# Hash-masked attention and a gated feed-forward layer on one core: value blocks 144 bytes apart, 128-row scores for ten head pairs, a new order of a few steps, and one more unit turned by DMA

## The chip, the core and the metric

The kernel runs on one NeuronCore of a Trainium2 chip. Five engines work side by side, each on its own in-order list of instructions: TensorE (PE in the profile, with its weight loads shown apart as PEld), VectorE (DVE), ScalarE (ACT), GpSimd (POOL) and SyncE (SP), which here only issues DMAs. They meet through semaphores. SBUF is the on-chip memory of 128 partitions, PSUM holds the matmul results, and DMAs move data between the external memory and SBUF or within SBUF. The metric is the device time of one execution in microseconds; of several executions the median counts.

## The reference

The input is q, k and v of shape 4 x 8 x 768 x 64 (batch, heads, tokens, head size), a projection of 64 x 6, and the weights of a feed-forward layer. All are float32, and the output is float32 of shape 3072 x 512. Cut to what matters:

```
q_bits = (q @ proj) > 0;  k_bits = (k @ proj) > 0            # six bits each
mask   = bucket(q_bits)[:, None] == bucket(k_bits)[None, :]   # same bucket only
scores = where(mask, q @ k.T / sqrt(64), -1e9)
attn   = exp(scores - max);  attn = attn / (sum(attn) + 1e-9)
x      = heads of (attn @ v) side by side                     # 3072 x 512
xn     = x / sqrt(mean(x * x) + 1e-6) * rms_g
out    = (silu(xn @ w_gate) * (xn @ w_val)) @ w_out           # 512 -> 1536 -> 512
```

## The kernel before, in words

**Units and slots.** The work is cut into eight units `w`: half of the tokens (384) of one batch `b = w // 2`. A unit's attention goes over 8 heads `h`, two heads forming a pair `hp`; its feed-forward part goes over 12 blocks `ft` of 128 of the 1536 hidden features. A list SLOTS (lines 33 to 36) holds 192 slots; a slot is one third of a head's scores, two blocks of 128 keys against 384 queries. Units 0 and 1 take turns by pairs, then units 2 and 3; units 4 to 7 follow one by one. A plan written out by hand (`at(slot, function, ..., rank=...)`, from line 595) puts every other step into a slot, and the loop from line 731 emits slot after slot: the next slot's scores, the steps with a rank below 3, the exponentials, then the other steps by rank. Each engine executes its own part in the order of this emission, so a step that waits holds up everything behind it on its engine.

**Scores.** For each pair a tile QK of 128 partitions holds, per head, the keys and the queries with the 64 head dimensions on partitions 0 to 63. Partitions 64 to 75 hold 12 rows of scaled hash bits, which make the matmul itself subtract a large number where the buckets differ, so KROWS = 76 rows are contracted (`k_cols`, `q_cols`, lines 146 to 157). The QK tiles come from a pool of six buffers (line 67). Rows 0 to 63 are written by casts (mostly on POOL, `cast_pool` and `cast_half`); the bit rows come by small DMAs on the SP queue or by copies on DVE. `scores` (line 343) issues two matmuls of 384 columns per slot, `probs` the exponential on ACT.

**Values.** `v_prep` (line 312) casts the values on POOL into the tile `vl` of shape 128 x 8 heads x 6 blocks x 66 in 16 bits, so one block starts 132 bytes after the one before; column 64 of each is one, which yields the sum of the exponentials. `av` (line 362) issues 18 matmuls per head, each with 65 columns of one such block moving, in two halves of nine. `v_sum` and `v_mean` form the mean of the values, from which `attn_out` takes the 1e-9 term.

**Output and norm.** `attn_out` (line 378; called through `o_step`) adds that term and divides on DVE, multiplies into x and squares, both on POOL; only for unit 0's last pair (`urgent`, line 392) do both run on DVE. `sumsq` (through `s_step`) sums the squares on DVE; `norm` (line 415) goes DVE, POOL, POOL. `scale_x` (DVE) and `turn_x` bring x into the layout for the next matmuls: for units in BY_DMA, here 3, 4 and 5, the first two of three chunks are turned by eight DMA transposes on the SP queue (line 441), otherwise by four TensorE transposes per chunk and a DVE multiplication (lines 448 and 449).

**Feed-forward.** Unit `w` starts its gate and value matmuls (lines 463 and 473) at slot 24w + 42 and its output matmuls (`project`, line 486) 16 slots later. `bank` hands out three PSUM banks for everything but scores and attention outputs: gates, values, output rows, transposes, hash products and value means all take their turn in them. A matmul into a bank waits until the engine that reads its former content has done so.

**Queue of SP.** All loads of q, k and v, the bit rows, the DMA transposes and the output rows are issued on the SP queue in the order of the plan. The weights are loaded from the POOL queue.

**The end.** The last 128 output rows are computed in two halves of 256 columns (lines 743 to 759): the first is copied by ACT and stored from SP; of the second ACT copies 128 columns and DVE the other 128 of the same bank, and ACT and SP store them.

## Time and profile before

| what | value |
| --- | --- |
| time, median of 3 runs | 334.26 us (334.0, 334.26, 335.18) |
| span of the profiled execution, first to last instruction | 332.5 us |
| time of the profiled execution itself | not listed apart from the three; the span is 1.8 us below their median |
| TensorE busy | 323.3 us, 97% of the span |
| VectorE, ScalarE, GpSimd busy | 234.2, 208.0 and 157.1 us (70%, 63%, 47%) |
| mean granted TensorE clock | 0.998 |
| DMA | 32.41 MB in 89956 packets |

How to read it: "busy" is the time in which at least one instruction of an engine was running. Matmuls overlap, so the duration of one (325 ns with 384 columns) is longer than the distance from its start to the start of the next. A group row of the profile gives line, engine, operation, tiles and shapes, count, then busy time in us and the mean of one in ns, then the idle time of the engine before these instructions and what ended it. A row of a timeline gives start and length in us; several like instructions in a row are merged, with their count. A row of a view by stretches gives the limits, the length, the busy time and count of each engine, the granted clock, the share of DMA time and GB/s. SPq rows are the issue of DMAs by SP, not their transfer.

### The profile page before, as it was taken

The page shows a single profiled execution, that of the slowest core. Times are in us where ns is not written, and L with a number is a line of the kernel's source. Part 1 is how long each engine was busy: PE and PEld are TensorE (multiplying, and loading weights), DVE is VectorE, ACT ScalarE, POOL GpSimd, SP SyncE. Part 2 cuts the span into 40 slices and gives each one's busy share as a digit, 9 for nine tenths or more (in the row PEclk, how much of TensorE's full clock was granted, in tenths as well). Part 3 has the DMA queues.
Part 4 walks back from the last instruction along what each step waited for, and adds up shares of the span by engine and source line. Part 5 has one row for each costly group of instructions (what it writes and reads, how often), then busy time and mean ns, then how long its engine had stood idle before and what let it go on. Part 6 is the DMA issues. An engine that isn't in the chain of part 4 may idle for free.

```text
span 332.5 us, 7788 instructions
## 1 busy us (share of the span) xinstructions
PE 323.3 (97%) x2959; PEld 198.5 (60%) x2959; DVE 234.2 (70%) x526; ACT 208.0 (63%) x324; POOL 157.1 (47%) x230
## 2 busy tenths in 40 slices
PE   8999989998999999999999999999999999999995
PEld 7576656555566556656565656566566656655653
DVE  3799579997598956989476874977257753793860
ACT  3788977674576665667675766757666766422421
POOL 4887956487747476376744365643110311130000
PEclk9999999999999999999999999999999999999999
DMA  6995997898348927841361714000200001002002
GB/s 221 349 201 151 147 173 140 158 172 134 117 86 156 168 40 174 156 90 24 91 146 34 141 34 150 3 17 18 80 32 2 3 32 65 0 3 82 13 2 95
DMA packets 89956, 32.41 MB, mean 97 GB/s; under 512 B 75336, under 2 KB 86848, under 8 KB 89920
## 3 DMA queue, kind: packets, MB, share of 16 engines
q1 hardware_dynamic: 85984, 27.14, 35.0%
q0 software_dynamic: 3712, 4.72, 9.2%
q8 instruction: 23, 0.38, 0.5%
q14 instruction: 13, 0.11, 0.1%
q10 hardware_dynamic: 224, 0.07, 0.1%
HBM read 28.58 MB, written 6.29 MB: 105 GB/s over the span
## 4 chain that ended last, share of the span: by engine, by line
PE 82%; DVE 5%; DMA 5%; POOL 4%; ACT 1%; issue 1%; SPq 1%; POOLq 0%; DVEq 0%; ACTq 0%
PE v_ps L473 17%; PE y_ps L486 16%; PE s_ps L348 15%; PE g_ps L463 14%; PE o_ps L370 9%; PE s_ps L463 4%; PE d_ps L214 3%; DMA QK<-bits 3%; PE t_ps L174 2%; DMA kL<-in_k_dram 1%; PE z_ps L341 1%; PE x_ps L448 1%; DVE t L474 1%; PE y_ps L747 1%; POOL sq L406 1%
## 5 line engine op out<-in xcount | busy, mean ns | idle before, releaser
L358 ACT ACTIVATE psb<-s_ps 128x768 f16<-128x768 f32 x192 | 150.6, 809 | 31.9 <-PE s_ps L348 29.9
L348 PE MATMUL s_ps<-QK 76*128 76x384 f16 x384 | 93.7, 325 | 2.5 <-DMA QK<-bits 1.3
L473 PE MATMUL v_ps<-xnT,wv 128*128 128x384 f16 x384 | 78.1, 325 | 0.0
L486 PE MATMUL y_ps<-wo,ht 128*128 128x512 f16 x276 | 69.2, 378 | 0.0
L394 POOL TENSOR_TENSOR x<-otmp,rcp 128x384 f32<-128x384 f32 x31 | 26.1, 843 | 84.8 <-DVE rcp L390 84.6
L370 PEld LDWEIGHTS <-psb 128*128 128x128 f16 x1152 | 52.2, 97 | 22.0 <-issue 3.6
L465 ACT ACTIVATE t<-g_ps 128x384 f32<-128x384 f32 x78 | 38.3, 491 | 43.2 <-PE g_ps L463 42.7
L463 PE MATMUL g_ps<-xnT,wg 128*128 128x384 f16 x312 | 63.4, 325 | 0.3
L474 DVE SCALAR_TENSOR_TENSOR t<-t,g_ps 128x384 f32<-128x384 f32 x78 | 42.7, 547 | 28.8 <-ACT t L465 28.4
L475 DVE SCALAR_TENSOR_TENSOR ht<-t,v_ps 128x384 f16<-128x384 f32 x96 | 53.2, 554 | 10.4 <-PE v_ps L473 0.9
L370 PE MATMUL o_ps<-vl,psb 128*128 128x65 f16 x1152 | 56.7, 193 | 0.3 <-DVE otmp L385 0.3
L463 PEld LDWEIGHTS <-wg 128*128 128x128 f16 x384 | 36.0, 97 | 24.1 <-issue 0.7
L473 PEld LDWEIGHTS <-wv 128*128 128x128 f16 x384 | 36.2, 97 | 23.2
L348 PEld LDWEIGHTS <-QK 76*128 76x128 f16 x384 | 31.3, 98 | 19.3 <-issue 4.7
L486 PEld LDWEIGHTS <-ht 128*128 128x128 f16 x276 | 26.0, 97 | 26.3 <-issue 1.9
L493 ACT COPY ysb<-y_ps 128x512 f32<-128x512 f32 x23 | 13.5, 587 | 24.6 <-PE y_ps L486 24.1
L406 POOL TENSOR_TENSOR sq<-x 128x384 f32<-128x384 f32 x31 | 26.3, 849 | 2.4
L385 DVE TENSOR_TENSOR otmp<-o_ps,cvb 128x390 f32<-128x390 f32 x32 | 17.9, 559 | 12.6 <-PE o_ps L370 12.5
L206 POOL CAST QK<-qT 64x768 f16<-64x768 f32 x22 | 18.1, 823 | 15.8 <-DVE qT L198 15.1
L206 POOL CAST QK<-kT 64x768 f16<-64x768 f32 x22 | 18.5, 841 | 13.6 <-PE m_ps L329 3.8
L449 DVE TENSOR_TENSOR xnT<-x_ps,gcol 128x512 f16<-128x512 f16 x18 | 12.2, 683 | 14.1 <-PE x_ps L448 14.0
L198 DVE STREAM_TRANSPOSE kT<-kL 128x192 f32<-128x192 f32 x44 | 21.7, 515 | 0.0
(81 smaller groups left out, 297.6 us busy)
## 6 DMA issues: line engine op xcount, KB each, us to landing
vL<-in_v_dram SPq DMA_DIRECT2D x16, 384.0 KB
out_dram<-ysb SPq DMA_DIRECT2D x23, 256.0 KB
kL<-in_k_dram SPq DMA_DIRECT2D x44, 96.0 KB
qL<-in_q_dram SPq DMA_DIRECT2D x44, 96.0 KB
kL<-in_k_dram SPq DMA_DIRECT2D x4, 384.0 KB
qL<-in_q_dram SPq DMA_DIRECT2D x4, 384.0 KB
wg<-in_moe_w_gate_dram POOLq DMA_DIRECT2D x2, 768.0 KB, 8.2
wv<-in_moe_w_val_dram POOLq DMA_DIRECT2D x2, 768.0 KB, 9.3
```

The costliest lines, as they stand in the source:

```text
L206: nc.gpsimd.tensor_copy(QK[b, hp][0:64, hh, o : o + S], T0[b, hp, which][64 * hh : 64 * hh + 64, :])
L348: nc.tensor.matmul(ps[:, j, 0:HALF], k_cols(w // 2, h, 2 * p + j), q_cols(w, h), start=True, stop=True,)
L358: nc.scalar.activation(psb[w, h][:, p], sps.pop(g)[:, :, 0:HALF], AF.Exp, scale=ESCALE,)
L370: nc.tensor.matmul(o[:, c, hh, 0:65], psb[w, h][:, jt // 2, jt % 2, 128 * c : 128 * c + 128], vls[b % 2][:, h, v_chunk(b, h, jt), 0:65], s ...
L394: eng.tensor_mul(xd.rearrange("p c (h d) -> p c h d", h=2), tmp[:, :, :, 0:64], r.to_broadcast([128, 3, 2, 64]),)
L406: nc.gpsimd.tensor_mul(sq, xd, xd)
L463: nc.tensor.matmul(g, wg[:, kt, fs], xnT[w][:, kt], start=(kt == 0), stop=(kt == 3))
L465: nc.scalar.activation(t, g, AF.Tanh, scale=0.5)
L473: nc.tensor.matmul(vv, wv[:, kt, fs], xnT[w][:, kt], start=(kt == 0), stop=(kt == 3))
L474: nc.vector.scalar_tensor_tensor(out=t, in0=t, scalar=1.0, in1=g, op0=ALU.add, op1=ALU.mult)
L475: nc.vector.scalar_tensor_tensor(out=ht[w][:, ft], in0=t, scalar=0.5, in1=vv, op0=ALU.mult, op1=ALU.mult)
L486: nc.tensor.matmul(y, ht[w][:, ft, c * 128 : (c + 1) * 128], wo[:, ft, :], start=(ft == 0), stop=(ft == NF - 1),)
```

## The change

- VSTEP = 72: the value blocks in `vl` lie 72 elements, 144 bytes, apart instead of 132. Reads still take 65 of them.
- The QK tiles are six fixed tiles `qkbuf` used in rotation, instead of six buffers of a pool. `clear_rows` sets partitions 64 to 127 of one of them to zero on POOL (a memset of 64 partitions x 1536 words): for buffers 4 and 5 at the start, behind the other memsets, and for buffers 2, 3, 0 and 1 in slots 76, 78, 97 and 98.
- For the ten pairs (1,0), (1,1) and all of batches 2 and 3, scores are contracted over all 128 rows instead of 76. Pairs of batch 0 and (1,2), (1,3) keep 76.
- `urgent` now covers unit 0's pairs 2 and 3: pair 2's multiplication and squares move from POOL to DVE, and its `s_step` goes.
- `s_step` of unit 6's last pair comes one slot earlier, and its `norm` two (slot 173 instead of 175).
- Unit 6 joins BY_DMA: chunks 0 and 1 are scaled in slots 175 and 176 together with the gain row, and are turned by eight DMA transposes on the SP queue in the same slots.
- `v_prep` and `v_sum` of pair (2,1) come two slots later (84 instead of 82), behind the norm of unit 2, which is planned in slot 83.
- `v_mean` of pairs 0 and 1 in batches 2 and 3 comes four slots earlier (88 instead of 92, and 136 instead of 140).
- The last 128 rows are computed in pieces of 256, 128 and 128 columns, each in a bank of its own. ACT copies and stores the first two; DVE copies the third, and SP stores it.

```
+VSTEP = 72
-BY_DMA = (3, 4, 5)
+BY_DMA = (3, 4, 5, 6)
-    qkpool = ctx.enter_context(tc.tile_pool(name="qkpool", bufs=6))
-    vls = [const.tile([128, H, 6, 66], FP16, name=f"vl{i}") for i in range(2)]
+    vls = [const.tile([128, H, 6, VSTEP], FP16, name=f"vl{i}") for i in range(2)]
+    qkbuf = [const.tile([128, 2, 2 * S], FP16, name=f"QK{i}") for i in range(6)]
-            QK[b, hp] = qkpool.tile([128, 2, 2 * S], FP16, name="QK")
+            QK[b, hp] = qkbuf[len(QK) % len(qkbuf)]
+    def clear_rows(i):
+        nc.gpsimd.memset(qkbuf[i][D:128].rearrange("p h n -> p (h n)").bitcast(FP32), 0.0)
+    def score_rows(b, hp):
+        return slice(0, 128 if (b, hp) in ((1, 0), (1, 1)) or b > 1 else KROWS)
-        return QK[b, h // 2][0:KROWS, h % 2, o : o + 128]
+        return QK[b, h // 2][score_rows(b, h // 2), h % 2, o : o + 128]
-        t = QK[b, h // 2][0:KROWS, h % 2]
+        t = QK[b, h // 2][score_rows(b, h // 2), h % 2]
-        urgent = (w, hp) == (0, 3)
+        urgent = (w, hp) in ((0, 2), (0, 3))
...
+    clear_rows(4)
+    clear_rows(5)
...
-        at(cast_slots[2], v_prep, b, hp)
-        at(cast_slots[2], v_sum, b, hp)
+        late = 2 if (b, hp) == (2, 1) else 0
+        at(cast_slots[2] + late, v_prep, b, hp)
+        at(cast_slots[2] + late, v_sum, b, hp)
         if b > 1 and hp % 2:
-            at(48 * b + (17 if hp == 3 else -4), v_mean, b, hp - 1, 4)
+            at(48 * b + (17 if hp == 3 else -8), v_mean, b, hp - 1, 4)
+    for i, s in ((2, 76), (3, 78), (0, 97), (1, 98)):
+        at(s, clear_rows, i, rank=6)
...
-                if (w, h) != (0, 7):
-                    late = 3 if h == 7 and w < 6 else 5 if (w, h) == (0, 5) else 4
-                    at(end + late, s_step, w, h // 2, rank=5 if late != 5 else 4)
+                if (w, h) not in ((0, 5), (0, 7)):
+                    late = 3 if h == 7 and w < 7 else 4
+                    at(end + late, s_step, w, h // 2, rank=5)
-        n0 = {0: 11, 2: 7, 3: 13, 4: 13, 5: 13}.get(w, 11)
+        n0 = {0: 11, 2: 7, 3: 13, 4: 13, 5: 13, 6: 13}.get(w, 11)
...
-    for i in range(2):
-        cs = slice(256 * i, 256 * i + 256)
+    for lo, hi in ((0, 256), (256, 384), (384, 512)):
         y = bank("y_ps")
...
+        copy, queue = (nc.vector.tensor_copy, nc.sync) if hi == 512 else (nc.scalar.copy, nc.scalar)
+        copy(ysb[:, lo:hi], y[:, lo:hi])
+        queue.dma_start(out=rows[:, lo:hi], in_=ysb[:, lo:hi])
```

More of the change, by code (lines that the diff above doesn't have):

```diff
@@ L747 @@
             nc.tensor.matmul(
-                y[:, cs], ht[7][:, ft, 256:384], wo[:, ft, cs],
+                y[:, lo:hi], ht[7][:, ft, 256:384], wo[:, ft, lo:hi],
                 start=(ft == 0), stop=(ft == NF - 1),
@@ L751 @@
         ysb = spool.tile([128, DMODEL], FP32, name="ysb", bufs=3)
-        if i == 0:
-            nc.scalar.copy(ysb[:, 0:256], y[:, cs])
-            nc.sync.dma_start(out=rows[:, cs], in_=ysb[:, 0:256])
-        else:
-            nc.scalar.copy(ysb[:, 0:128], y[:, 256:384])
-            nc.vector.tensor_copy(ysb[:, 128:256], y[:, 384:512])
-            nc.scalar.dma_start(out=rows[:, 256:384], in_=ysb[:, 0:128])
-            nc.sync.dma_start(out=rows[:, 384:512], in_=ysb[:, 128:256])
+        copy, queue = (nc.vector.tensor_copy, nc.sync) if hi == 512 else (nc.scalar.copy, nc.scalar)
+        copy(ysb[:, lo:hi], y[:, lo:hi])
+        queue.dma_start(out=rows[:, lo:hi], in_=ysb[:, lo:hi])
 _INS = ['q', 'k', 'v', 'proj', 'moe_w_gate', 'moe_w_val', 'moe_w_out', 'moe_rms_g']
```

## The prediction

> **What bounds the kernel now.** I read the page's busy times first, then the view by stretches, then what TensorE waits for.

> ```profile
> PE 323.3 (97%) x2959; PEld 198.5 (60%) x2959; DVE 234.2 (70%) x526; ACT 208.0 (63%) x324; POOL 157.1 (47%) x230
> 46.00:76.60 30.60, 29.33 (x283) 17.82 (x280) 27.43 (x64) 20.36 (x32) 20.60 (x29) 1.00 0.87 154
> 76.60:122.00 45.40, 44.76 (x409) 26.45 (x410) 34.31 (x78) 28.91 (x44) 28.67 (x39) 1.00 0.60 117
> 122.00:285.00 163.00, 162.71 (x1493) 98.86 (x1492) 111.50 (x235) 108.70 (x168) 70.73 (x92) 1.00 0.30 67
> ```

> The first numbers behind the length are TensorE's. From 76.6 us to 285 us it stands idle for 0.93 us in all, and no other engine comes near it: work taken off TensorE there shortens the run by its full amount. Before 76.6 us that does not hold:

> ```profile
> 75.27 0.44 PE L370 MATMUL o_ps<-vl,psb 128*128 128x65 f16 x9
> 76.65 0.48 PE L348 MATMUL s_ps<-QK 76*128 76x384 f16 x2 [0.94 <-DMA QK<-bits]
> 64.41 0.68 DVE L221 TENSOR_SCALAR bits<-d_ps,thr,scl 128x384 f16<-128x384 f32 x1
> 68.61 0.58 SPq L116 DMA_DIRECT2D vL<-in_v_dram  x1
> 69.29 6.20 SPq L289 DMA_DIRECT2D QK<-bits  x8
> 70.99 5.53 DMA QK<-bits
> ```

> The nine attention matmuls that start at 75.27 are streamed by 75.55 (31 ns each, below), and the next scores start at 76.65: 1.1 us of waiting for the hash bits of pair (1,1). DVE had these bits at 65.09, but SP is behind with loads and reaches their DMAs only at 69.29; the third, issued at 70.99, lands 5.53 us later. SP and the transfers set this moment, not TensorE. What TensorE gains ahead of it only lengthens the wait, and I count nothing of it.

> **The value blocks.** Mean distance between attention matmuls after 76.6 us (first row: those of line 370 alone):

> ```profile
> 76.60:332.50 255.90, 40.54 (x819) 37.62 (x819) 1.00 0.31 70
> 77.84 0.43 PE L370 MATMUL o_ps<-vl,psb 128*128 128x65 f16 x9
> L370 PE MATMUL o_ps<-vl,psb 128*128 128x65 f16 x1152 | 56.7, 193 | 0.3 <-DVE otmp L385 0.3
> L448 PE MATMUL x_ps<-ident,xn 128*128 128x128 f16 x72 | 7.0, 219 | 1.2 <-DVE xn L434 1.2
> ```

> 819 matmuls are 91 runs of nine like the second row; a run is eight distances and one duration of 193 ns, so a distance is (40.54 - 91 x 0.193) / 728 = 31.6 ns. The transposes, in 18 runs of four, give (7.0 - 18 x 0.219) / 54 = 56.6 ns for 128 columns, 28.7 ns for 65. Sorted by where the block starts, the single start times behind the first row say the same: 29.2 ns from a block whose address is a multiple of 16 bytes (each fourth), mostly 32 to 35 ns from the others. With 144 bytes all are multiples. 819 x (31.6 - 29.2) = 1.9 us, all on TensorE after 76.6; 0 if the address is not the reason, 819 x (31.6 - 28.7) = 2.4 at most. I take 1.9, the value that the aligned blocks show now.

> **128-row scores.** A matmul's length does not depend on the rows:

> ```profile
> L348 PE MATMUL s_ps<-QK 76*128 76x384 f16 x384 | 93.7, 325 | 2.5 <-DMA QK<-bits 1.3 <-ACT psb L358 0.8 <-ACT qT L182 0.2
> L473 PE MATMUL v_ps<-xnT,wv 128*128 128x384 f16 x384 | 78.1, 325 | 0.0
> ```

> Both last 325 ns. But in the start times behind these rows the first matmul of a score pair takes 165 to 167 ns to the next start and the first one after the pair 3 to 4 ns above its usual distance, where steps between other 128-row groups cost nothing. Per pair that is 7.6 ns; 108 of the 132 pairs after 76.6 us change to 128 rows: 0.8 us. I take it; the other end is 0, if the switch is owed to something else. More rows cannot cost anything that these rows show.

> **Unit 6 by DMA.** Eight transposes go: 8 x 56.6 ns = 0.45 us. DVE loses two multiplications and gets two longer scalings, about even. On SP eight transposes are new:

> ```profile
> 227.00 10.05 SPq L441 DMA_TRANSPOSE xnT<-xn  x8
> L441 SPq DMA_TRANSPOSE xnT<-xn x24: 1131/1230/2083, 152.2 to 235.8; - x24
> 262.34 0.55 DVE L410 TENSOR_REDUCE ssp<-sq 128x3 f32<-128x384 f32 x1
> 258.05 0.83 POOL L406 TENSOR_TENSOR sq<-x 128x384 f32<-128x384 f32 x1
> 278.39 0.81 PE L463 MATMUL g_ps<-xnT,wg 128*128 128x384 f16 x4
> ```

> The squares are there at 258.9, so the sum, now one slot (1.3 us) earlier, runs at about 261.0, the root is there at 263, the first scaling ends at about 264.7. Eight issues take 10.05 to 12 us and the last lands some 2.3 us after its issue (their completions in the trace), so 276 to 277.5. Unit 6's first gate matmul would come at about 277.9: a margin of 0.4 to 2 us. Queued behind on SP are only unit 5's output rows, which have three buffers. I count the 0.45.

> **Norm of unit 2 and the means.**

> ```profile
> 116.45 0.82 POOL L314 CAST vl<-vL 128x768 f16<-128x768 f32 x1
> 118.84 0.46 POOL L322 TENSOR_TENSOR vsum<-vadd 128x128 f16<-128x128 f32 x1
> 119.66 0.86 POOL L423 TENSOR_TENSOR rstd<-ms,mhalf 128x3 f32<-128x3 f32 x1
> 120.02 0.49 PE L348 MATMUL s_ps<-QK 76*128 76x384 f16 x2
> 121.10 0.40 PE L448 MATMUL x_ps<-ident,xn 128*128 128x128 f16 x4 [0.59 <-DVE xn L434]
> 131.91 0.45 PE L370 MATMUL o_ps<-vl,psb 128*128 128x65 f16 x9
> 132.50 0.81 PE L463 MATMUL g_ps<-xnT,wg 128*128 128x384 f16 x4
> ```

> TensorE could go on at 120.02 + 0.33 and starts at 121.10: 0.75 us. The root stands on POOL behind the value steps of 116.45 to 119.3; behind it they move, and it ends near 118.1, some 2.4 us earlier. Late next are the value sums, done near 121, ahead of the mean in slot 88 at about 124. The whole 0.75 goes. The gate at 132.50 waits 0.3 us (131.91 + 0.28 to 132.50) for the third bank, one of three being held by the mean just before it; the mean of batch 3 is followed by the same wait. Moved, these two give 0.6, less about 0.2 if in slot 88 the mean meets a bank that ACT still copies: 0.4.

> **Clears, the first norm, the end.**

> ```profile
> L518 POOL MEMSET pq<- 128x48 f32 x1 | 0.1, 149 | 0.0
> masks.py:197 POOL MEMSET ident<- 128x128 f32 x1 | 0.2, 204 | 0.3 <-POOLq L774 0.3
> L533 POOL MEMSET vl<- 128x48 f16 x2 | 0.6, 396 | 0.0
> 5.51 1.06 POOL L190 CAST QK<-kT 64x384 f16<-64x384 f32 x2 [2.10 <-DVE kT L182]
> 8.83 0.49 PE L348 MATMUL s_ps<-QK 76*128 76x384 f16 x2 [0.20 <-ACT qT L182]
> 113.01 0.83 POOL L394 TENSOR_TENSOR x<-otmp,rcp 128x384 f32<-128x384 f32 x1 [4.31 <-DVE rcp L390]
> 141.44 1.70 POOL L206 CAST QK<-qT 64x768 f16<-64x768 f32 x2 [3.58 <-DVE qT L198]
> 40.63 0.55 DVE L410 TENSOR_REDUCE ssp<-sq 128x3 f32<-128x384 f32 x1 [1.54 <-POOL sq L406]
> 329.08 0.27 ACT L756 COPY ysb<-y_ps 128x128 f32<-128x128 f32 x1 [0.94 <-PE y_ps L747]
> 329.38 0.29 DVE L757 COPY ysb<-y_ps 128x128 f32<-128x128 f32 x1 [7.06 <-ACT ysb L756]
> ```

> Contiguous memsets cost (204 - 149) / 80 = 0.7 ns per element: 149 + 1488 x 0.7 = 1.2 us for a clear. The first two fill the 2.1 us that POOL waits ahead of the cast at 5.51, the rest delays it by about 0.4; the first scores come at 8.83, when that cast would have been done for 1.8 us. At the strided row's 396 / 48 = 8.2 ns it would be 12.7 us each; I take 1.2, since the cleared words are contiguous. The other four, in pairs of 2.4 us, come just ahead of idle times of POOL of 4.3 us (to 113.01) and 3.6 us (to 141.44). They cost 0; without that idle time a clear would put off the x and the casts behind it by its 1.2 us.

> The first norm gets about 1.4 us earlier: POOL's multiplication and squares of pair 2, on which DVE waits 1.5 us, go to an idle DVE. It lies before 76.6 us and counts 0 by itself.

> At the end DVE's copy need not follow ACT's in one bank, so the last store starts 0.3 us earlier, less 0.05 for 24 short matmuls in place of 12: 0.25.

> **The longer wait and the clock.** With 1.4 from the norm, some 0.5 from the value blocks (an estimate from the distances above), and less than all of it should DVE then meet loads that have not landed, the wait of 1.1 us at 76.65 grows to some 2.5. The trace shows one idle stretch as long:

> ```profile
> 327.92:331.33 3.41, 1.08 (x10) 0.72 (x8) 0.29 (x1) 0.49 (x2) 0.00 (x0) 1.00 0.44 151
> 331.33:332.50 1.17, 0.00 (x0) 0.00 (x0) 0.00 (x0) 0.00 (x0) 0.00 (x0) 0.50 0.00 0
> ```

> After 3.41 us with only 1.08 us of work the granted clock is 0.50. If 2.5 us of idle fall into such a window, TensorE runs at half speed for one window: 3.41 / 2 = 1.7 us lost. The ends are 0 and 1.7, about one execution in two meets the window, and I take 0.9 for the median. [...]

> **The sum.** 1.9 + 0.8 + 0.45 + 0.75 + 0.4 + 0.25 = 4.6 us off, 0.9 on: 3.7. The profiled span becomes 328.8. It lies 1.8 below the median of the runs, 334.26, and I let that stay: 330.6 us.

> **Rivals.** (a) The bits come as much earlier as TensorE does: then 1.6 us before 76.6 count too and the clock holds: 334.26 - 4.6 - 1.6 = 328.1. For it speaks only that SP waits on compute now and then, against it the unbroken issue rows up to 75.5. (b) The address is not what matters. [...] As a mechanism: no 1.9, 332.5 us. The sorted distances speak against it. (c) Unit 6's transposes land after the gate is due, as with the slowest row (2.08 us) repeated: 1 to 2 us lost, 331.6 to 332.6. (d) Slower: POOL clears at the strided rate. Two cost 25.4 us, POOL's first casts end at 3.4 + 25.4 + 1.1 = 29.9, the scores of 8.83 come 21 us late; if the wait at 76.65 hides 2.5 of it, 330.6 + 18.5 = 349. It begins to cost above 2.1 us a clear (8.75 - 3.4 - 1.06 over two) and decides the sign above about 5. Against it stands the contiguous row. That alignment and rows both do nothing gives 333.3, no change.

> **How the numbers follow.** Forecast 0.71, with 329.6 to 331.6 around it (clock never or always, rows not paying); (a) 0.07, (b) 0.07, (c) 0.08, (d) 0.04, no change 0.03. Half a per cent, 1.7 us, is what a measurement here can tell from none: below 332.6 is faster. Forecast, (a), most of (c), half of (b) and a little doubt on all: faster 0.86, same 0.08, slower 0.06. The range goes from between (a) and the forecast to (b): 328.8 to 332.6.

> **What would show it.** Line 370's matmuls 29 ns apart; scores of the ten pairs 162 ns apart at both ends; no wait at line 448 near 120 us; the wait for QK bits of (1,1) near 76.6 us longer, about 2.5 us, and the clock below 1.00 behind it or not; no gate waiting for the transposes of unit 6; clears of 1.2 us. I am wrong if the bits move with TensorE, if line 370 stays at 31 ns, or if a new wait of over 1 us stands after 76.6 us.

## The result and the profile after

The changed kernel takes 332.6 us (median of 22 executions, 329.55 to 336.88) against 334.1 us of the kernel before in the same series (22 executions, 332.7 to 336.28). The ratio of the times (changed to before) is 0.9931, with a 95% interval from 0.991 to 0.9952: about 0.7% faster. It leaves out the slow executions, of the changed kernel the five from 334.52 us up; the two medians alone, over all executions, give 0.9955. The forecast was 330.6 us, 3.7 us less than before; 1.5 us came, and the median lies on the upper end of the forecast range, 332.6 us. The profiled execution of the changed kernel is the slowest of its 22, at 336.88 us (span 335.1 us), so its trace is read for the places of the loss, and the sizes are taken from pieces of it that run at full clock and from the experiments.

The page's busy times and the view by stretches (columns: stretch, its length, busy time of PE, PEld, DVE, ACT and POOL with instructions, granted clock, DMA share, GB/s), changed kernel:

```profile
PE 323.8 (97%) x2963; PEld 199.2 (59%) x2963; DVE 236.1 (70%) x530; ACT 207.8 (62%) x324; POOL 164.5 (49%) x234
74.74:78.15 3.41, 0.68 (x11) 0.41 (x9) 3.41 (x8) 0.00 (x0) 3.29 (x4) 1.00 0.88 166
78.15:81.56 3.41, 2.12 (x6) 0.87 (x7) 0.87 (x2) 0.81 (x1) 2.68 (x5) 0.50 0.19 34
81.56:84.98 3.42, 3.42 (x18) 1.64 (x17) 0.00 (x0) 0.97 (x2) 0.00 (x0) 0.50 0.88 139
84.98:122.00 37.02, 37.00 (x346) 22.34 (x345) 29.50 (x66) 23.51 (x38) 22.84 (x28) 1.00 0.65 125
122.00:285.00 163.00, 162.99 (x1505) 99.02 (x1504) 111.75 (x235) 110.50 (x171) 76.89 (x98) 1.00 0.31 69
```

From 85 us on TensorE stands idle for 0.03 us in 200 (0.93 us between 76.6 and 285 us before). All the trouble lies in three clock windows ahead of it: one with 0.68 us of work, then two at half clock. A window is here a piece of 3.413 us counted from a change of the granted clock: in this trace the clock changes at 78.15, 84.98 and 334.15 us, and 6.83 and 249.17 us are 2 and 73 times 3.413.

The timeline of the changed kernel around slot 60, and the places that the forecast named (columns: start, length, engine, line, operation, tiles, count, and in brackets the idle time before it with what the profile takes for its releaser):

```profile
68.98 0.89 POOL L552 DMA_DIRECT2D wo<-in_moe_w_out_dram  x1
69.54 0.58 SPq L117 DMA_DIRECT2D vL<-in_v_dram  x1
70.22 9.22 SPq L296 DMA_DIRECT2D QK<-bits  x8
74.98 0.44 PE L377 MATMUL o_ps<-vl,psb 128*128 128x65 f16 x9
79.44 0.80 PE L355 MATMUL s_ps<-QK 128*128 128x384 f16 x2 [4.02 <-POOL vsum L329]
3.46 2.69 POOL L139 MEMSET QK<- 64x1536 f32 x2
266.51 11.02 SPq L448 DMA_TRANSPOSE xnT<-xn  x8
281.19 0.81 PE L470 MATMUL g_ps<-xnT,wg 128*128 128x384 f16 x4
331.93 0.29 DVE L765 COPY ysb<-y_ps 128x128 f32<-128x128 f32 x1 [6.87 <-DMA out_dram<-ysb]
332.25 0.33 SPq L766 DMA_DIRECT2D out_dram<-ysb  x1
```

The attention matmuls of 74.98 are streamed by 75.26, and the next scores start at 79.44: 4.2 us of idle time where 1.1 us stood before and 2.5 us were forecast. The profile names POOL's value sum, which writes nothing that these scores read; the third of the eight bits DMAs in the row above was issued at 72.28 and landed at 79.30 us, 7.0 us later, and that is what the scores read. The eight issues took 9.22 us (6.20 before). The clears cost 1.34 us each, and the first scores come at 8.90 us in place of 8.83; over all profiled executions here they come at 7.9 to 9.2 us, with the clears and without, so these two figures show no cost.

The grouped rows (columns: busy time and mean of one in ns, then idle time of the engine ahead of them and its releaser) show no wait at the transposes of line 455, where 1.2 us stood before, and none at the attention matmuls:

```profile
L377 PE MATMUL o_ps<-vl,psb 128*128 128x65 f16 x1152 | 56.3, 194 | 0.0
L455 PE MATMUL x_ps<-ident,xn 128*128 128x128 f16 x64 | 6.2, 219 | 0.0
```

By start times, the stretch from slot 66 (behind the half clock) to slot 191 took 198.21 us before and 195.52 us after, 2.69 us less. Other traces repeat both figures: 198.19 us in the kernel before with the earlier norm alone, which changes nothing there, and 195.48 to 195.59 us in six of the seven runs below that keep all of the change behind slot 66 and insert nothing there (196.24 us in the first run with wo in slot 42). The forecast for the same stretch was 1.9 + 0.8 + 0.45 + 0.75 + 0.4 = 4.3.

### The profile page after: what moved, and what is told of

It reads as the page before. It is cut to its first block, busy times and chain, and to the rows that moved or that the text cites. A ratio compares the mean times of both kernels' runs of the same rounds, so it can differ in the third digit from the quotient of the medians.

```text
span 335.1 us, 7835 instructions
## 1 busy us (share of the span) xinstructions
PE 323.8 (97%) x2963; PEld 199.2 (59%) x2963; DVE 236.1 (70%) x530; ACT 207.8 (62%) x324; POOL 164.5 (49%) x234
## 4 chain that ended last, share of the span: by engine, by line
PE 89%; POOL 4%; DVE 2%; DMA 1%; ACT 1%; SPq 1%; issue 1%; DVEq 0%; POOLq 0%; ACTq 0%
PE y_ps L493 18%; PE s_ps L355 18%; PE v_ps L480 18%; PE g_ps L470 14%; PE o_ps L377 10%; PE d_ps L221 4%; PE s_ps L470 3%; PE t_ps L181 2%; ACT psb L365 1%; PE z_ps L348 1%; PE x_ps L455 1%; POOL QK L213 1%; DMA kL<-in_k_dram 1%; SPq L127 1%; DMA out_dram<-ysb 1%
## 5 line engine op out<-in xcount | busy, mean ns | idle before, releaser
L355 PE MATMUL s_ps<-QK 128*128 128x384 f16 (+1 forms) x384 | 94.5, 328 | 6.3 <-POOL vsum L329 4.0
L480 PE MATMUL v_ps<-xnT,wv 128*128 128x384 f16 x384 | 78.1, 326 | 0.0
L493 PE MATMUL y_ps<-wo,ht 128*128 128x512 f16 x276 | 71.0, 387 | 0.0
L355 PEld LDWEIGHTS <-QK 128*128 128x128 f16 (+1 forms) x384 | 31.2, 98 | 23.5 <-issue 4.9
L493 PEld LDWEIGHTS <-ht 128*128 128x128 f16 x276 | 26.7, 99 | 27.5 <-issue 3.8
L413 POOL TENSOR_TENSOR sq<-x 128x384 f32<-128x384 f32 x30 | 25.5, 850 | 2.4
L456 DVE TENSOR_TENSOR xnT<-x_ps,gcol 128x512 f16<-128x512 f16 x16 | 10.9, 685 | 17.5 <-PE x_ps L455 17.4
```

The costliest lines, as they stand in the source:

```text
L355: nc.tensor.matmul(ps[:, j, 0:HALF], k_cols(w // 2, h, 2 * p + j), q_cols(w, h), start=True, stop=True,)
L413: nc.gpsimd.tensor_mul(sq, xd, xd)
L480: nc.tensor.matmul(vv, wv[:, kt, fs], xnT[w][:, kt], start=(kt == 0), stop=(kt == 3))
L493: nc.tensor.matmul(y, ht[w][:, ft, c * 128 : (c + 1) * 128], wo[:, ft, :], start=(ft == 0), stop=(ft == NF - 1),)
```

## The experiments

My theory after the result: two terms behind slot 66 are smaller than forecast, and the wait at slot 60 is longer because the bits of pair (1,1) come later than before, beside the load of the second half of wo. The rivals: the clock alone is what costs (the wait is harmless), SP's backlog of loads sets the bits and not wo, or the earlier first norm is the cause.

**Clock or wait.** Extra matmuls fill the idle time; their result is not used.

```
-        idle(ps[:, 0, HALF:512], {0: 8, 3: 6}.get(g, 0))
+        idle(ps[:, 0, HALF:512], {0: 8, 3: 6, 60: 66}.get(g, 0))
```

> The changed kernel with 66 extra matmuls of 128 columns (their result is not used) on TensorE just ahead of the scores of slot 60, where the changed kernel idles for 4.18 us; 66 x 56.7 ns = 3.7 us. Nothing else changes. If the halved clock behind that idle time is what keeps the changed kernel above the forecast, the granted clock is 1.00 in every execution and the median goes from 332.6 to about 330.6, with all executions within about 1.5 us of each other. If the clock is halved for another reason, or if the halving is not what costs the time, the median stays near 332.6 and single executions reach 335 or more.

Measured: 332.82 us (12 executions, 332.03 to 335.26; ratio to the kernel before of that series 0.9954, 0.9922 to 0.9986), and a mean granted clock of 0.998 to 1.000 in all twelve; of the 22 executions of the changed kernel 15 lay below 0.996. Its timeline:

```profile
74.44 3.85 PE L348 MATMUL s_ps<-ones 128*128 128x128 f16 x66
79.49 0.48 PE L355 MATMUL s_ps<-QK 128*128 128x384 f16 x2 [1.20 <-POOL QK L213]
```

So the idle time does halve the clock (0.50 from 78.15 us on in the changed kernel), and work in it keeps the clock up (1.00 from 74 to 80 us here). The median did not fall to 330.6, though. A likely reason, which no run separates, is that the filler holds TensorE for 3.7 us in every execution, also where the bits would have come sooner, and gives away what the clock gains. The clock is one part of the matter; the wait itself is another, and in this profiled execution the bits landed no earlier (79.35 us) than in that of the changed kernel.

**The second wo load.** It is issued in slot 42 in place of 52; run in two series.

```
-        at(36 + 16 * i, load_wo, 6 * i, 6 * i + 6)
+        at(36 + 6 * i, load_wo, 6 * i, 6 * i + 6)
```

> The changed kernel with the second half of wo (768 KB) issued in slot 42, near 55 us, where the DMA engines are 0.45 busy, in place of slot 52, near 69 us. If the bits of pair (1,1) land late because that load drains beside them, they land at about 76.5 us or earlier in place of 79.3, the wait of TensorE at slot 60 falls from 4.2 us to 1.5 to 2 us, the clock is halved seldom, and the median is 328.5 to 330. If SP reaching those DMAs late (at 70.2 us) is the cause, the wait stays at about 4 us and the median near 332.5. If the load in its new place holds up the key and query loads of pair (1,2), DVE waits for them near 62 us and the bits come later still: above 333.

> The changed kernel with the second half of wo in slot 42 alone, once more: it was the fastest so far at 330.18, but over 6 executions. Beside it in this series stand the kernel before and the version with both loads moved and the old norm. If the wo move carries the gain, 330 to 330.8 again, 1.1% below the kernel before, and the wait at slot 60 is 1 us or less; if the first result was chance, 331.5 and a wait of 2 us or more.

Measured: 330.18 us (6 executions, 329.76 to 334.67; ratio to the kernel before 0.989, 0.9835 to 0.9944), and 330.40 us (6 executions, 329.58 to 331.67; ratio 0.9895, 0.9871 to 0.9918). The timeline of the second run:

```profile
69.16 6.19 SPq L296 DMA_DIRECT2D QK<-bits  x8
73.69 0.44 PE L377 MATMUL o_ps<-vl,psb 128*128 128x65 f16 x9
73.96 0.49 PE L355 MATMUL s_ps<-QK 128*128 128x384 f16 x2
84.64 0.49 PE L355 MATMUL s_ps<-QK 76*128 76x384 f16 x2 [1.56 <-DMA QK<-bits]
```

SP reaches the bits 1.1 us earlier (69.16 against 70.22 us), the eight issues take 6.19 us, each DMA lands 4.2 to 1.8 us after its issue, and there is no wait at slot 60, nor is there one in the trace of the first run (the 0.9 us that an expectation further down gives for it stands at slot 66). The third DMA lands at 73.71 us, 5.6 us earlier than in the changed kernel; 1.4 us of that is its earlier issue, and the rest is the shorter way from issue to landing. So it is mainly the load of wo that holds these bits up, not SP's backlog. The backlog sets what is late next, the bits of pair (1,2): 1.56 us at 84.64. This version is 1.1% faster than the kernel before. Against the change as it was made it gains 2.2 us by the medians and 1.2 us by the ratios; no other kernel here was faster in the median.

**The values of pair (1,3) behind the bits.**

```
-        (1, 3): in_row((38, 40, 44), 56, 65),
+        (1, 3): in_row((38, 40, 53), 56, 65),
```

> The changed kernel with the load of the values of pair (1,3) (384 KB) in slot 53, behind the bits of pair (1,1) on SP, in place of slot 44. 384 KB at the 190 GB/s of that stretch are 2.0 us. If the transfers ahead of and beside the bits set the wait, the bits land about 2 us earlier, the wait at slot 60 falls from 4.2 us to 1.5 to 2.5 us and the median is 329 to 330.5. If the large wo load alone does it, the wait falls by the 0.6 us that SP gains, and the median is about 332. If the values then come too late for their own step in slot 65, a wait of POOL and of the means shows behind slot 64, and nothing is gained.

Measured: 331.51 us (6 executions, 329.19 to 333.6; ratio 0.9897, 0.9844 to 0.995). In its profile the wait at slot 60 is 2.1 us, the eight issues take 6.91 us, the third DMA lands at 76.89 us, and the clock stays at 1.00. The wait lies between that of the changed kernel and none, as expected of transfers beside the bits; the time can't be told from that of the wo move.

**Both loads moved,** with the changed kernel's first norm and with the one before.

> The changed kernel with both moves: the second half of wo in slot 42 and the values of pair (1,3) in slot 53. Each alone cut the wait at slot 60 (4.2 us in the profile of the changed kernel) to 0.9 and 2.1 us. If transfers ahead of and beside the bits set the wait, together they leave 0 to 1 us, the clock is 1.00 in nearly all executions, and the median is 329 to 330 with less spread. If the wait then passes to the key loads of pair (1,2) or to DVE, the median is that of the wo move alone, 330.2.

> The changed kernel with both loads moved and the first norm as it was before. Against the changed kernel with both loads moved (330.85) this shows what the earlier norm is worth once the transfers ahead of slot 60 are lighter. If TensorE is then the bound throughout, the earlier norm counts its 1.2 us, and this kernel takes about 331.5 to 332; if the bits still set slot 60, the two are alike; if the earlier norm costs even here, this one is the faster, 330 or less.

Measured: 330.85 us (6 executions, 329.19 to 331.75; ratio 0.9886, 0.9849 to 0.9923) with the earlier norm, 331.08 us (6 executions, 330.73 to 331.62; ratio 0.9913, 0.9897 to 0.9929) with the old one. No wait is left at slot 60 in either trace (9.35 us from slot 54 to slot 60 in both, as in every trace here without that wait). Moving both loads can't be told from moving wo alone (0.9886 against 0.989 and 0.9895), and what the earlier norm is worth once the transfers are out of the way stays inside the intervals: 0 to some 1 us, not shown.

**The earlier first norm,** taken out of the changed kernel, and put alone into the kernel before.

```
-        urgent = (w, hp) in ((0, 2), (0, 3))
+        urgent = (w, hp) == (0, 3)
...
-                if (w, h) not in ((0, 5), (0, 7)):
-                    late = 3 if h == 7 and w < 7 else 4
-                    at(end + late, s_step, w, h // 2, rank=5)
+                if (w, h) != (0, 7):
+                    late = 3 if h == 7 and w < 7 else 5 if (w, h) == (0, 5) else 4
+                    at(end + late, s_step, w, h // 2, rank=5 if late != 5 else 4)
```

> The changed kernel with the first norm as it was before: pair 2 of unit 0 goes through POOL again, and its row sum stands where it stood. TensorE then comes to the scores of slot 60 about 1.2 us later. If the earlier norm only lengthens the wait there, as forecast, the wait is about 1.2 us shorter, the second half of the run starts at the same time, the clock is halved less often, and the median is 331 to 332.5. If the earlier norm also sends the first wo load and what follows earlier and so holds up the loads of pair (1,1), the bits land near 76.5 us again, the wait is 1 to 1.5 us, and the median is about 330: the earlier norm would then cost 2 us. If the earlier norm is a gain that counts in full, the median is about 333.8.

> The kernel before with the earlier first norm alone (pair 2 of unit 0 on DVE like pair 3, its row sum without a step of its own). Slot 42 then comes about 1.2 us earlier. If the bits of pair (1,1) do not move with TensorE, the wait at slot 60 takes all of it: 334.1, or up to 335 where the clock is halved behind it. If the earlier first wo load makes the bits later, 335 or more in the median. If TensorE's gain counts, 332.9. Undoing the same edit in the changed kernel took 1.1 us off, so I expect 334.1 to 335.2.

Measured: without it 331.54 us (6 executions, 330.53 to 331.71; ratio 0.9912, 0.9879 to 0.9946). By the medians that is 1.1 us less than the changed kernel, by the ratios (0.9912 against 0.9931) 0.6 us, with intervals that overlap; the two were measured in different series. Alone in the kernel before, 335.56 us against 333.95 (12 and 21 executions; ratio 1.0044, 1.0016 to 1.0071): slower by 1.6 us, which is clear of the noise. The timelines, first the kernel before with the earlier norm alone, then the changed kernel without it:

```profile
67.74 0.89 POOL L543 DMA_DIRECT2D wo<-in_moe_w_out_dram  x1
68.34 0.58 SPq L116 DMA_DIRECT2D vL<-in_v_dram  x1
69.02 9.59 SPq L289 DMA_DIRECT2D QK<-bits  x8
76.50 0.48 PE L348 MATMUL s_ps<-QK 76*128 76x384 f16 x2 [2.29 <-DMA QK<-bits]
78.08 0.59 PE L486 MATMUL y_ps<-wo,ht 128*128 128x512 f16 x2 [0.66 <-DMA wo<-in_moe_w_out_dram]
87.92 0.49 PE L348 MATMUL s_ps<-QK 76*128 76x384 f16 x2 [1.46 <-DMA QK<-bits]
```

```profile
66.35 0.58 SPq L117 DMA_DIRECT2D vL<-in_v_dram  x1
67.04 6.85 SPq L296 DMA_DIRECT2D QK<-bits  x8
68.53 0.89 POOL L552 DMA_DIRECT2D wo<-in_moe_w_out_dram  x1
75.03 0.44 PE L377 MATMUL o_ps<-vl,psb 128*128 128x65 f16 x9
75.30 0.49 PE L355 MATMUL s_ps<-QK 128*128 128x384 f16 x2
```

The rows show an order of two transfers. SP, which issues the values and the bits, is behind with its loads; the wo load is issued by POOL. With the earlier norm the 768 KB go out ahead of the bits instead of about level with them or behind them. Over the profiled executions, with the wo load issued in slot 52 and the values where they were (the first scores of these executions come at 8.1 to 9.0 us, so differences of some tenths between rows mean nothing):

| kernel | wo issued, us | bits from, us | eight issues, us | third landed, us | slot 60 at, us |
|---|---|---|---|---|---|
| before | 68.75 | 69.29 | 6.20 | 76.52 | 76.65 |
| before, 128 rows alone | 67.94 | 68.39 | 6.20 | 75.18 | 75.32 |
| before, value blocks alone | 68.31 | 68.65 | 6.50 | 77.15 | 77.28 |
| before, order and unit 6 | 68.79 | 67.46 | 6.20 | 73.59 | 75.60 |
| changed, old norm | 68.53 | 67.04 | 6.85 | 72.37 | 75.30 |
| before, earlier norm alone | 67.74 | 69.02 | 9.59 | 76.36 | 76.50 |
| changed | 68.98 | 70.22 | 9.22 | 79.30 | 79.44 |
| changed, filler | 68.17 | 69.58 | 9.70 | 79.35 | 79.49 |
| changed, matmuls added at slots 90 to 110 | 67.16 | 68.25 | 7.43 | 76.34 | 76.47 |

Where wo goes out 1.2 us or more ahead of the bits, the eight issues take over 9 us; at 1.1 us ahead (the last row) 7.4; where it goes out 0.3 to 0.5 us ahead of them or behind them, 6.2 to 6.9. The last two rows and "changed" and "before, earlier norm alone" have the earlier norm, the other five the old one.

The loss need not show at slot 60. In the trace of the earlier norm alone slot 60 starts no later than before (76.50 against 76.65 us), though TensorE waits 2.29 us there in place of 0.94 (both by the profile's rows). But the eight issues end 3.1 us later and put off what SP issues behind them: TensorE waits 0.66 us for wo itself and 1.46 us for the bits of pair (1,2), and slot 66 starts at 87.92 us, where it stood at 85.63 before.

What brings wo ahead of the bits is only in part shown. Counted from the first scores, the wo load of slot 52 goes out at 59.1 to 60.1 us with the earlier norm and at 59.8 to 60.2 us with the old one, hardly earlier, because it stands on POOL behind other steps (busy without a gap from 64.28 us to the load at 68.75 before, from 64.51 to 68.98 in the changed kernel); SP reaches the bits at 60.2 to 61.3 us against 58.7 to 60.5 us, later by 1 us in the mean. A likely reason for the second is the first half of wo, in slot 36. With the earlier norm it goes out 1.0 to 1.9 us earlier, by the same count, and SP takes 1.4 to 3.3 us, in place of 0.6 to 1.8, to issue the values of pair (1,1) behind it. First the kernel before, then the changed one:

```profile
44.75 0.99 POOL L543 DMA_DIRECT2D wo<-in_moe_w_out_dram  x1
46.19 1.76 SPq L116 DMA_DIRECT2D vL<-in_v_dram  x1
```

```profile
43.71 0.99 POOL L552 DMA_DIRECT2D wo<-in_moe_w_out_dram  x1
46.17 2.99 SPq L117 DMA_DIRECT2D vL<-in_v_dram  x1
```

The expectations above name this rival; no run moved the first half of wo, so its share stays open.

**The parts behind slot 66, one by one.** First the value blocks alone, in the kernel before:

```
+VSTEP = 72
...
-    vls = [const.tile([128, H, 6, 66], FP16, name=f"vl{i}") for i in range(2)]
+    vls = [const.tile([128, H, 6, VSTEP], FP16, name=f"vl{i}") for i in range(2)]
```

> The kernel before with value blocks 144 bytes apart and nothing else changed. The forecast had 1.9 us for it (31.6 to 29.2 ns per matmul, 819 of them): 332.2. The profile of the changed kernel shows 29.2 ns at seven of nine positions and some 35 ns at two, 30.5 on average: 819 x 1.1 ns = 0.9 us, 333.2. If the address is not the reason for the shorter distances: no change, 334.1. The wait at slot 60 should grow by the 0.5 us that is gained ahead of it, and not more.

Measured: 333.51 us (12 executions, 331.73 to 336.79; ratio 0.9969, 0.9934 to 1.0004, an interval that includes no change). From slot 66 to slot 191 the trace has 197.65 us against 198.21. Then the 128 rows alone, that is the parts of the change's diff that name qkbuf, clear_rows and score_rows:

> The kernel before with the ten pairs' 128-row scores alone: six fixed buffers, the clears, 128 rows in both operands. The forecast had 7.6 ns for each of 108 pairs, 0.8 us, so 333.3 against 334.1. The profile of the changed kernel shows 5 of these 7.6 ns gone, 0.55 us: 333.6. If the switch of rows is not the reason, the first score of a pair stays at 166 ns and the time at 334.1. If fixed buffers add waits that the pool did not have, 334.5 or more.

Measured: 334.34 against 334.18 us (12 and 17 executions; ratio 1.0005, 0.9974 to 1.0036), no difference that can be measured; in the trace 197.84 us against 198.21. Then the order of value steps and means with unit 6 by DMA:

```
-BY_DMA = (3, 4, 5)
+BY_DMA = (3, 4, 5, 6)
...
+        late = 2 if (b, hp) == (2, 1) else 0
+        at(cast_slots[2] + late, v_prep, b, hp)
+        at(cast_slots[2] + late, v_sum, b, hp)
...
-            at(48 * b + (17 if hp == 3 else -4), v_mean, b, hp - 1, 4)
+            at(48 * b + (17 if hp == 3 else -8), v_mean, b, hp - 1, 4)
```

> The kernel before with the order of the value steps of pair (2,0) and (2,1), the means and unit 6 by DMA alone; no other blocks, no 128 rows, the first norm as it was. All of it lies behind 76.6 us on TensorE: forecast 0.75 for the norm of unit 2, 0.4 for the means, 0.45 for unit 6, together 1.6: 332.5. The profile of the changed kernel shows these three at 0.75, 0.45 and 0.46. If one of them needs the others parts of the change, or comes back as a new wait, the time lies above 333.

Measured: 332.73 us against 333.95 (10 and 21 executions; ratio 0.996, 0.9936 to 0.9983), and in the trace 196.57 us against 198.21, 1.64 us: 0.89 around slot 88, 0.30 around slot 134, 0.45 between slots 180 and 191. The three traces give 0.56 + 0.37 + 1.64 = 2.57 us of the 2.69 that the whole change shows there.

**The distance of short matmuls.** In the changed kernel seven of nine positions in a run of attention matmuls are 29.2 ns from the next and two, the second and the seventh, 35. To see whether that belongs to the value blocks, three groups of 40 extra matmuls of 65 columns read one contiguous tile, from byte 0, 2 and 4 of its row (result not used):

```
+        for o in {90: [0] * 40, 100: [1] * 40, 110: [2] * 40}.get(g, []):
+            nc.tensor.matmul(ps[:, 0, HALF : HALF + 65], ones16, ones16[:, o : o + 65], start=True, stop=True)
```

> The changed kernel with 40 extra matmuls of 65 columns (result not used) on TensorE ahead of the scores of slots 90, 100 and 110. All read one contiguous tile; the moving block starts at byte 0, 2 and 4 of its row. If a start off the 16-byte line costs the time, the first 40 are 29 to 30.5 ns apart and the other two groups 32 to 35. If the address is not the reason, all three are alike. If the 35 ns that the changed kernel shows at two positions of each nine belong to a run of short matmuls as such, they recur about every fifth in the first group; if they belong to the attention blocks, the first group is 29 ns throughout.

The single execution took 336.52 us. Its timeline:

```profile
126.23 1.38 PE L355 MATMUL s_ps<-ones 128*128 128x65 f16 x40
143.68 1.41 PE L355 MATMUL s_ps<-ones 128*128 128x65 f16 x40
160.44 1.36 PE L355 MATMUL s_ps<-ones 128*128 128x65 f16 x40
```

A group is 39 distances and one duration of 193 ns: 30.4, 31.2 and 29.9 ns. In the first group the single distances are 29 or 30, with a 35 at every fifth; in the second a 35 at every third; in the third a 32 at every fourth. So in this execution a run from byte 0 has a regular long step of its own, and holds 30.4 ns. And a start that is no multiple of 16 bytes was not slow as such: the third group, from byte 4, is the fastest.

## Why the prediction was right or wrong

The direction and the reason for most of the gain were right; the forecast median was 2.0 us too low. That the measured median still lies in the range, on its very end, is luck: the range went up to 332.6 us for value blocks that bring nothing; they brought a part of their term, and terms outside that case failed as well. Behind slot 66 the change brings 2.7 us and not 4.3, and ahead of it the wait costs more than forecast, and for a cause that was not forecast.

**The value blocks** are the term that was most mis-sized: 1.9 forecast. The cleanest pair of rows is that of two experiments at full clock, order and unit 6 alone and then the changed kernel with the old norm, both over 825 attention matmuls:

```profile
75.60:330.30 254.70, 40.73 (x825) 37.66 (x821) 1.00 0.32 71
75.30:328.40 253.10, 39.98 (x825) 37.13 (x821) 1.00 0.33 72
```

0.75 us: from 31.4 to 30.4 ns by the prediction's own formula, and 0.56 us between slots 66 and 191 in the trace of the blocks alone. The step that failed is "the value that the aligned blocks show now". In the old kernel an aligned block follows steps of 32 to 35 ns; 29.2 ns is a distance that single steps reach between longer ones, and no run here holds it. The run from byte 0 in the distance experiment shows the same 30.4 without any value block. What about the address makes a run slower stays open, since the start at byte 4 was not slow there. Rival (b), no gain at all, would have left the distance unchanged and does not agree with these traces, though the time of the blocks alone does not exclude it.

**128 rows** were forecast at 0.8 us. The reason was right: the first score of a pair goes from 166 to 163 ns, the first gate or value step behind it from 165.4 to 162.9, the first projection step from 218.6 to 215.9. These are means of the start times between slots 66 and 191, before and with the 128 rows alone. But of 7.6 ns some 5 to 6 go, and the other steps grow by 0.3 to 0.5 ns each (gate and value 161.9 to 162.3, projections 215.4 to 215.9), so 0.37 us is left in the trace, too little for the times to show. "More rows cannot cost anything that these rows show" was the step that failed: 0.3 to 0.5 ns on many hundred steps does not show in a rounded row.

**Norm of unit 2, means, unit 6, end.** 0.75, 0.4, 0.45 and 0.25 were forecast. Measured: 0.89 around slot 88 (that wait gone, and one of the two at the third bank), 0.30 for the other mean, 0.45. The transposes of unit 6 were issued until 277.5 us, landed at 278.6, and no gate waited; rival (c) did not come. At the end the last store follows the last matmul's start by 0.71 us (331.54 to 332.25) in place of 0.97; the 24 short matmuls take 0.04 us of that back. These steps held.

**Clears** cost 1.34 us each against 1.2 forecast, and nothing that shows at the first scores. Rival (d) fell.

**The first norm** is the step that failed in kind. "It lies before 76.6 us and counts 0 by itself" left out what else changes its place with it: POOL's loads of wo. With the earlier norm the load of slot 52 goes out ahead of the bits that SP issues, SP's issues take longer, and these bits or those of the next pair come later. The norm costs 1.6 us alone and 0.6 to 1.1 us in the change, where I had 0.9 for the longer wait and the clock together. Rival (a), bits that come earlier with TensorE, did not come: in the changed kernel they came later. The wait was forecast at 2.5 us, and the profiled execution shows 4.2.

**The clock** was forecast as one window lost in about one execution of two. It was more: 15 of 22 executions lay below 0.996, and the profiled one lost two windows. The seven executions at 0.999 or more take 329.55 to 331.2 us, with a median of 330.6, and the fifteen take 331.7 to 336.88 us, with a median of 333.18. The earlier norm alone shows the same split: six of its twelve executions lie below 0.996, with a median of 336.4 us, and the other six have 334.0, about that of the kernel before in that series. So most of what the norm costs lies in executions whose clock is halved; but one at full clock, the profiled one at 336.76 us, lost as much by its waits alone. Whether the waits were longer in the halved executions, too, is not known. That a window with a little work is enough is borne out. Windows of 3.41 us with 0.68 (changed kernel) and 1.41 us of work (value blocks alone, the first row below; its wait at slot 60 had grown to 2.0 us) are followed by one at half clock, and one with 1.75 us (values of (1,3) moved, the second row) is not:

```profile
74.31:77.73 3.42, 1.41 (x16) 0.83 (x14) 3.42 (x8) 0.00 (x0) 3.30 (x5) 1.00 0.68 117
```

```profile
75.35:78.77 3.42, 1.75 (x17) 1.08 (x18) 3.12 (x6) 0.81 (x1) 3.20 (x5) 1.00 0.55 145
```

The sum of the parts closes to 0.4 us: 334.1 less 2.69 less 0.22 at the end is 331.19, and the changed kernel without the earlier norm takes 331.54. What is left up to 332.6 us, 1.1 us, is put down to the norm by difference alone.

## What to carry to other kernels

A step that only brings work forward is not free because a wait swallows it: list what else is issued by the slots that come earlier, on every queue, and ask which small transfer a bulk load now goes ahead of. A distance that single instructions reach between slower neighbours (29.2 ns here) is not a rate that a run of them holds (30.4 ns here); take the price of a regular run from a regular run. Before giving TensorE a longer wait, look at its clock windows: behind one with 2 us of idle time (value blocks alone) a window of 3.41 us ran at half clock, by estimate another 1.7 us lost. In the changed kernel four output matmuls took 1.91 us at half clock (from 80.03 us) and 1.03 us at full clock (from 85.33 us).
